# Attention and MoE on one core: a head's row maxima are transposed and stored in the following head's slot, and v's magnitude is broadcast one slot later

## The chip, the cores and the metric

The kernel runs on one core of a Trainium2 chip. The metric is the device time of one execution in microseconds (us); the time of before is the median of three runs. Besides, one execution was recorded by the hardware profiler, and all views quoted here are of that execution. PE is the engine for matrix products, PEld its weight loads, DVE, ACT and POOL are the vector, scalar and general engines, SP only issues transfers. "ACTq" is the instruction queue of ACT where it issues a transfer.

## The reference, cut to what matters

```python
# q, k, v: 8 batches, 8 heads, 576 rows of 64; block = 64
scores = scale * np.matmul(q, k.transpose(0, 1, 3, 2))
scores = np.where(block_i >= block_j, scores, -1000000000.0)
scores = scores - np.max(scores, axis=-1, keepdims=True)
attn = np.exp(scores)
attn = attn / (np.sum(attn, axis=-1, keepdims=True) + 1e-09)
out = np.matmul(attn, v)
# x: the heads side by side, 4608 tokens of 512
h = x @ w_in                                  # 512 -> 2048
sp = np.maximum(h, 0.0) + np.log1p(np.exp(-np.abs(h)))
g = h * erf(sp)
return g @ w_out                              # 2048 -> 512
```

So there are 64 heads of masked attention, and behind them one feed-forward layer over 4608 tokens.

## The kernel before

**Attention, one head after the other.** A loop over n runs through 64 heads and four slots more. One turn of the loop is called a slot here. In slot n the code lists the steps of several heads and merges them evenly over the slot:

- `load_qk(n + 3)` brings the queries and keys of head n + 3 into one of four buffers `qk`.
- `maxes(n + 2)` finds the row maxima of head n + 2: five groups of score products `s` on PE (L324), each reduced by DVE into a column of `mx` (L327), and then step `e`. Step `e` takes the smaller of two columns on DVE (L352), transposes `mx` on PE into `mt` (L354), copies that row out of PSUM on ACT (L356), and has ACT issue a transfer that puts it into a row of the head's `qk` buffer (L357).
- `probs(n)` computes the scores of head n once more (`t`, L370 and L371; L370 reads the stored row, which subtracts the maximum), takes the exponential on ACT (L375), and splits the result in two float16 parts `ph` and `pl` (L381 on ACT, L382 on DVE).
- `pv` multiplies two heads' probabilities by v (`u`, L414) and sums them (`us`, L437); `normalise` does the rest for four heads (`rt`, `rb`, `xs`).

Every fourth slot `load_v` fetches v of four heads, and in the slot after it `prep_v` takes its largest magnitude (`vm` on DVE, transposed to `vt` on PE, three small DVE instructions on `vs`), broadcasts it by a PE product `vb` (L284), copies that as `vsb` and scales v into `vh` and `vl`.

**Feed-forward as filler.** The first 6 of 16 chunks of the feed-forward width (`F1`) are computed in units of 256 tokens and two chunks: 24 products `m_h` (L154), the gate on ACT, DVE and POOL (L123 to L137), and 12 products `o` (L164), which is 36 PE matmuls a unit and 54 units in all. The tokens of a batch are ready when its eight heads are done. The other ten chunks (`m2`) follow at the end, in tiles of 512 tokens.

**What sets the order.** The code gives an order of priority, and when the program is built a list scheduler lays down every engine's rows: where it reckons an engine free, it puts a later instruction that is ready, mostly of the filler, ahead. On the chip every engine then works through its own rows strictly in that order, and a row that has to wait holds up all rows behind it. `late(kind, ...)` shifts a step's priority; the kinds that the change touches have no shift. PSUM tiles come from four rotating banks (`bank`, pool `ps_a`), plus the filler's own while there is no filler yet. Until then PE also gets `warm` products without a use.

Of the kernel before, what the change touches and what calls it, by code (L numbers as in the profile page):

```python
# [15 lines left out]
AX = mybir.AxisListType  # L16
# the top word of the float64 2**-126, read as a float32
LEAST = 0.25 * (1 + 0.125) * 2.0**-13
PSUM = bass.MemoryType.PSUM

# erf(softplus(h)) as a function of r0 = tanh(T0 * h + T1).  Each step makes the next r:
#   ("S", i):    (p[0] * r_i + p[1]) ** 2
#   ("M", i, j): (r_i + p[0]) * r_j
#   ("A", i, j): p[0] * r_i + r_j
# and the value is the last r plus FIN.
PROG = [('S', 0), ('S', 1), ('M', 2, 2), ('M', 1, 3), ('M', 4, 4)]
# [8 lines left out]
def tile_attention_moe(ctx: ExitStack, tc: tile.TileContext, qk, v, w, maskrows, sels, out):  # L35
    nc = tc.nc
    B, H, D2, S = qk.shape
# [5 lines left out]
    F1 = 6  # L43
    SP = 640
    SCALE = 0.125
    NQ = H // 4
# [42 lines left out]
    def load_weight(whi, wlo, stage, f):  # L89
        """the two float32r parts of chunk f of both weights, out of the words of their float64"""  # L90
        for s in range(2):
            nm = f"{f}_{s}"
            raw = stage[0][0].tile([P, stage[0][2]], I32, tag=stage[0][1][s], bufs=stage[0][3], name=f"raw{nm}")[:, : 2 * DM].rearrange("p (n t) -> p n t", t=2)
            nc.sync.dma_start(raw.rearrange("p n t -> p (n t)"), w[f, s].bitcast(I32))
            top, low = raw[:, :, 1], raw[:, :, 0]
            # sign, exponent and 20 bits of mantissa as a float32 (0 for what is below its range)
            bits = stage[1][0].tile([P, stage[1][2]], I32, tag=stage[1][1], bufs=stage[1][3], name=f"bits{nm}")[:, :DM]
# [4 lines left out]
            nc.vector.scalar_tensor_tensor(out=sq, in0=sq, scalar=LEAST * LEAST, in1=f32(bits), op0=ALU.is_ge, op1=ALU.mult)  # L102
            # the low word, of the weight that the exponent gives it
            nc.vector.tensor_scalar(out=bits, in0=sq.bitcast(I32), scalar1=-0x800000, scalar2=None, op0=ALU.bitwise_and)  # L104
# [8 lines left out]
    def gate(h, name, gpool):  # L113
        """g = h * erf(softplus(h)) as a sum of two float32r parts"""
        n = h.shape[1]
        last = {}
# [26 lines left out]
    def moe_unit(ws, xh, xl, o, tw, nu, u, name, first, last, spread):  # L143
        """nu chunks of d_ff over tw tokens: the steps to their g, and those to their part of o"""
        turns.append(u)
# [25 lines left out]
    def merged(*lists):  # L171
        """the steps of all lists, each list (steps, from, to) spread evenly over its part of the whole"""
        order = []
        for n, (steps, lo, hi) in enumerate(lists):
            order += [(lo + (hi - lo) * (i + 0.5) / len(steps), n, i) for i in range(len(steps))]
        return [lists[n][0][i] for _, n, i in sorted(order)]
# [4 lines left out]

# [1 line left out]
    def load_x(pool, t, tw):  # L183
# [33 lines left out]
    def moe1(ready, lag):  # L217
        """the next step of the first F1 chunks, if there is one: a unit up to its g together with an earlier unit from g on"""
        t = len(xs1)
# [19 lines left out]
    with tc.tile_pool(name="apool", bufs=2) as apool, tc.tile_pool(name="spool", bufs=1) as spool, \  # L239
# [4 lines left out]
        nc.sync.dma_start(sel, sels)  # L244
        # columns of the keys' tiles 0, 3, 4 and 1, 2 in the two parts of a head's probabilities
        p32s = [spool.tile([P, n], F32, name=f"p32_{i}") for i, n in enumerate(PN)]
# [10 lines left out]
        def bank(name):  # L257
            """a bank of PSUM; all of them take part as long as the other chunks of d_ff need none"""
            turn.append(0)
            k = len(turn) % 8 if not xs1 else 0  # L260
            if k in (2, 5):
                return ps_h.tile([P, 512], F32, tag="h", name=name)
            if k in (3,):
                return ps_o.tile([P, 512], F32, tag="o", name=name)
            return ps_a.tile([P, 512], F32, tag="a", name=name)
# [5 lines left out]

        def prep_v(b, qd, v32):
            """two float16 parts of v over its largest magnitude, and that magnitude"""
            nm = f"{b}_{qd}"
# [3 lines left out]
            nc.tensor.transpose(out=pt[:1, :P], in_=vm, identity=ident)  # L278
            vs = apool.tile([1, 2], F32, tag="vs", name=f"vs{nm}")
            nc.vector.tensor_reduce(out=vs[:, :1], in_=pt[:1, :P], axis=AX.X, op=ALU.max)  # L280
            nc.vector.tensor_scalar(out=vs[:, :1], in0=vs[:, :1], scalar1=1e-30, op0=ALU.max, scalar2=None)
            nc.vector.reciprocal(out=vs[:, 1:2], in_=vs[:, :1])
            pb = bank(f"vb{nm}")
            nc.tensor.matmul(pb[:, :2], lhsT=onesrow, rhs=vs, start=True, stop=True)  # L284
# [11 lines left out]
        def part(n, i):  # L296
            """part i of head n: kl over kh, qh over ql, kh over 5 rows that mask, qh over 5 rows that mask"""
            return qks[n % NB][:, i * S : (i + 1) * S]
# [18 lines left out]
        def maxes(n):  # L317
            """the steps to the rows' maxima, negated, in the row of t that goes with the ones"""
            mx, K = mxs[n % 2], D + 4
# [41 lines left out]
        def probs(n, out):  # L361
            """the steps to exp(0.125 * s - its maximum), keys on partitions, in two float16 parts"""
            K = D + 5
# [25 lines left out]
        def pv(qd, pp, prs, V, usb, rs):  # L389
            """the steps to the unnormalised outputs of heads 2pp and 2pp+1 of the quad, and to their sums"""  # L390
            vsb, vh, vl = V
            st = {}

            def ranges(q0, q1):
                """keys' tiles that a part of the queries attends to: the queries, and where their probabilities are"""
                for j in range(5):
# [21 lines left out]

            # the sums of two heads' first 384 and last 192 queries, in a group of 32 columns each
            order = []  # L420
# [24 lines left out]
        def normalise(b, qd, usbs, rs):  # L445
            nm = f"{b}_{qd}"
            # pair, tile of the sums, part of the queries, head
            ri = apool.tile([P, 2, 3, 2, 2], F32, tag="ri", name=f"ri{nm}")
# [29 lines left out]
        for n in range(NB - 1):  # L478
            for f in load_qk(n):
                f()  # L480
        v32 = load_v(0, 0)
        vs[0] = prep_v(0, 0, v32)
        for f in maxes(0) + maxes(1):
            f()
        def late(kind, steps):
            """steps whose instructions the scheduler holds behind the next ones of the order, or ahead of some (offsets in instructions)"""
            def run(f):
# [27 lines left out]
        for n in range(N + 4):  # L515
# [4 lines left out]
            if n + 2 < N:  # L520
                lists.append((late("max", maxes(n + 2)), 0, 1))
            if n < N:
# [3 lines left out]
            if n % 4 == 1 and qd < N // 4:  # L526
                v32 = load_v(*divmod(qd, NQ))
            if n % 4 == 2 and qd < N // 4:
                lists.append((late("v", [lambda qd=qd: vs.__setitem__(qd, prep_v(*divmod(qd, NQ), v32))]), 0, 1))
            if n % 2 == 0 and 2 <= n <= N:  # L530
# [26 lines left out]

# [1 line left out]
    N2 = 2  # L559
# [89 lines left out]
```

## Time and profile before

| | |
|---|---|
| time, median of 3 runs | 1394.77 us (1393.82 to 1400.65) |
| span of the profiled execution | 1407.0 us; no other time is given of that execution |
| attention with filler, from head 12 to the first score product of head 63 | 170 to 743 us |
| filler alone, then the weights of the other chunks | 743 to about 960 us |
| the other chunks | to the end |

Three views are used: busy time by stretch of the span (with the granted clock of PE, 1.00 being full speed), the waits of an engine by what it waited for, and the instructions in order of time. An engine's idle time counts only where something behind it is late because of it. A busy PE need not be a PE at its peak, since matmuls are pipelined and their ends modelled.

### The profile page before, as it was taken

The page shows a single profiled execution, that of the slowest core. Times are in us where ns is not written, and L with a number is a line of the kernel's source. Part 1 is how long each engine was busy: PE and PEld are TensorE (multiplying, and loading weights), DVE is VectorE, ACT ScalarE, POOL GpSimd, SP SyncE. Part 2 cuts the span into 40 slices and gives each one's busy share as a digit, 9 for nine tenths or more (in the row PEclk, how much of TensorE's full clock was granted, in tenths as well). Part 3 has the DMA queues.
Part 4 walks back from the last instruction along what each step waited for, and adds up shares of the span by engine and source line. Part 5 has one row for each costly group of instructions (what it writes and reads, how often), then busy time and mean ns, then how long its engine had stood idle before and what let it go on. Part 6 is the DMA issues. An engine that isn't in the chain of part 4 may idle for free. (4 is left out here: it accounts for less than half of the span.)

```text
span 1407.0 us, 21952 instructions
## 1 busy us (share of the span) xinstructions
PE 1273.8 (91%) x8198; PEld 1026.1 (73%) x8198; DVE 1013.9 (72%) x1525; ACT 793.2 (56%) x1493; POOL 602.1 (43%) x454
## 2 busy tenths in 40 slices
PE   3798789989899898999889898779999999999998
PEld 1455567777777787777777787568888888888887
DVE  5768997788878788788697648996555555564654
ACT  1456566667666676667567455544444454445453
POOL 3757665445554554544445424562222222222221
PEclk9879899999999999999999899899999999999999
DMA  8557655757657576566623542302211311321110
GB/s 228 135 125 204 173 156 137 185 154 193 179 129 207 146 196 175 152 161 177 174 81 137 188 164 95 130 0 78 102 60 68 113 60 60 108 72 61 60 61 30
DMA packets 89370, 179.95 MB, mean 128 GB/s; under 512 B 8540, under 2 KB 27292, under 8 KB 89264
## 3 DMA queue, kind: packets, MB, share of 16 engines
q1 hardware_dynamic: 79280, 159.41, 38.1%
q0 software_dynamic: 9344, 18.97, 6.1%
q8 instruction: 65, 1.06, 0.3%
q10 hardware_dynamic: 640, 0.17, 0.1%
q14 instruction: 41, 0.34, 0.1%
HBM read 112.29 MB, written 37.75 MB: 107 GB/s over the span
## 5 line engine op out<-in xcount | busy, mean ns | idle before, releaser
L130 DVE SCALAR_TENSOR_TENSOR m_r<-m_r 128x512 f32<-128x512 f32 x288 | 232.9, 809 | 229.3 <-ACT m_r L128 225.8
L137 POOL TENSOR_TENSOR m_gl<-m_r,m_gh 128x512 fp32r<-128x512 f32 x144 | 195.5, 1357 | 443.7 <-ACT m_gh L136 359.2
L136 ACT CAST m_gh<-m_r 128x512 fp32r<-128x512 f32 x144 | 89.2, 619 | 251.9 <-DVE m_r L135 251.7
L154 PE MATMUL m_h<-xh,whi 128*128 128x256 f32 (+1 forms) x648 | 213.3, 329 | 17.3 <-DVE m_r L135 17.3
L128 ACT ACTIVATE m_r<-m_r,c 128x512 f32<-128x512 f32 x288 | 207.9, 722 | 11.0 <-ACT m_r L128 0.4
L154 PE MATMUL m_h<-xl,whi 128*128 128x256 f32 (+1 forms) x648 | 211.1, 326 | 0.3 <-DMA xl<-x_d 0.3
L154 PE MATMUL m_h<-xh,wlo 128*128 128x256 f32 (+1 forms) x648 | 211.1, 326 | 0.0
L327 DVE TENSOR_REDUCE mx<-s 64x1 f32<-64x288 f32 (+4 forms) x384 | 167.9, 468 | 56.4 <-PE s L324 53.9
L375 ACT ACTIVATE p<-t 128x288 f32<-128x288 f32 (+4 forms) x384 | 143.1, 388 | 97.9 <-PE t L371 76.2
L164 PE MATMUL o<-whi,m_gh 128*128 128x512 f32 x432 | 173.8, 403 | 6.7 <-ACT ob L209 4.3
L164 PE MATMUL o<-wlo,m_gh 128*128 128x512 f32 x432 | 173.8, 402 | 0.0
L382 DVE TENSOR_TENSOR pl<-p,ph 128x832 f16<-128x832 f32 (+1 forms) x128 | 158.5, 1240 | 18.0 <-ACT ph L381 17.8
L312 POOL TENSOR_TENSOR qk<-st,qk 64x576 fp32r<-64x576 f32 x64 | 103.2, 1613 | 157.5 <-PE s L324 55.9
L154 PEld LDWEIGHTS m_h<-xh,whi 128*128 128x128 f32 x648 | 126.6, 195 | 37.8 <-DVE m_r L135 21.9
L164 PE MATMUL o<-whi,m_gl 128*128 128x512 f32 x432 | 153.0, 402 | 0.2 <-POOL m_gl L137 0.2
L370 PE MATMUL t<-qk 69*128 69x288 f32 (+4 forms) x384 | 136.0, 355 | 12.6 <-DVE mx L327 7.0
L324 PE MATMUL s<-qk 68*128 68x256 f32 (+3 forms) x384 | 126.6, 362 | 14.3 <-DVE mx L327 8.7
L313 POOL TENSOR_TENSOR qk<-st,qk 64x576 fp32r<-64x576 f32 x64 | 111.3, 1739 | 65.5 <-DMA qk<-qk 61.7
L154 PEld LDWEIGHTS m_h<-xl,whi 128*128 128x128 f32 x648 | 126.5, 195 | 15.8 <-DMA xl<-x_d 0.6
L154 PEld LDWEIGHTS m_h<-xh,wlo 128*128 128x128 f32 x648 | 126.9, 196 | 9.4
L371 PE MATMUL t<-qk 128*128 128x288 f32 (+4 forms) x384 | 129.8, 339 | 0.0
L123 ACT ACTIVATE m_r<-m_h,c 128x512 f32<-128x512 f32 x144 | 98.8, 686 | 50.5 <-PE m_h L154 48.7
(84 smaller groups left out, 2499.1 us busy)
## 6 DMA issues: line engine op xcount, KB each, us to landing
st<-qk SPq DMA_DIRECT2D x64, 288.0 KB
qk<-qk POOLq DMA_DIRECT2D x64, 288.0 KB, 4.6
qk<-qk SPq DMA_DIRECT2D x64, 288.0 KB
x_d<-xs SPq DMA_DIRECT2D x32, 576.0 KB
raw<-w SPq DMA_DIRECT2D x32, 512.0 KB
v<-v SPq DMA_DIRECT2D x16, 640.0 KB
qk<-qk SPq DMA_DIRECT2D x64, 144.0 KB
xh<-x_d SPq DMA_DIRECT2D x18, 512.0 KB
```

What stands on the lines that cost most here:

```text
L128: nc.scalar.activation(r, regs[o[1]], AF.Square, bias=const(pp[1]), scale=pp[0])
L130: nc.vector.scalar_tensor_tensor(out=r, in0=regs[o[1]], scalar=pp[0], in1=regs[o[2]], op0=ALU.add, op1=ALU.mult)
L137: nc.gpsimd.tensor_tensor(out=gl, in0=g, in1=f32(gh), op=ALU.subtract)
L154: nc.tensor.matmul(h[:, k, :], lhsT=a[:, 0, sl], rhs=x[:, cc, :], start=cc == 0 and i == 0, stop=cc == NCC - 1 and i == 2)
L164: nc.tensor.matmul(o[c], lhsT=a[:, sl], rhs=b_[:, 1, :], start=first and k == 0 and not lo and b_ is whi, stop=last and k == nu - 1 and lo)
L313: nc.gpsimd.tensor_tensor(out=t[D:, 1, :], in0=st[D:, :], in1=f32(t[D:, 1, :]), op=ALU.subtract)
L324: nc.tensor.matmul(dst[:r, :w_], lhsT=qh[:K, i * P : i * P + r], rhs=kh[:K, k0 : k0 + w_], start=True, stop=True)
L327: nc.vector.tensor_reduce(out=mx[:r, col : col + 1], in_=src, axis=AX.X, op=ALU.max, negate=True)
L370: nc.tensor.matmul(s[:kk, :w_], lhsT=kh[:K, ks], rhs=qh[:K, q0 : q0 + w_], start=True, stop=False)
L371: nc.tensor.matmul(s[:kk, :w_], lhsT=klh[:, ks], rhs=qhl[:, q0 : q0 + w_], start=False, stop=True)
L375: nc.scalar.activation(p32s[part][:kk, c : c + w_ - skip], s[:kk, skip:w_], AF.Exp, scale=SCALE)
L382: nc.vector.tensor_tensor(out=pl, in0=p, in1=ph, op=ALU.subtract)
```

## The change

Step `e` of `maxes(n + 2)` no longer stands at the end of slot n. It is kept in `rows` and listed in slot n + 1, spread over the first 0.6 of it; probs of that head still stand in slot n + 2. `prep_v` is cut in two: `scale_v` ends with the reciprocal in `vs` and stays in the slot of before, and the rest, from the broadcast `vb` on, comes one slot later. What is computed, and how often, stays the same. (Comments and docstrings also go, which moves line numbers: L324, L327, L352, L354, L356, L357 and L370 become L332, L335, L360, L362, L364, L365 and L378; L284 becomes L292.)

```diff
+        vs_ = {}
+        def scale_v(b, qd, v32):
             nm = f"{b}_{qd}"
             vm = apool.tile([P, 1], F32, tag="vm", name=f"vm{nm}")
...
             vs = apool.tile([1, 2], F32, tag="vs", name=f"vs{nm}")
+            vs_[qd + NQ * b] = vs
             nc.vector.tensor_reduce(out=vs[:, :1], in_=pt[:1, :P], axis=AX.X, op=ALU.max)
...
             nc.vector.reciprocal(out=vs[:, 1:2], in_=vs[:, :1])
+
+        def prep_v(b, qd, v32):
+            nm = f"{b}_{qd}"
+            vs = vs_.pop(qd + NQ * b)
             pb = bank(f"vb{nm}")
...
+        scale_v(0, 0, v32)
         vs[0] = prep_v(0, 0, v32)
-        for f in maxes(0) + maxes(1):
-            f()
+        rows = {}
+        for n in range(2):
+            *steps, rows[n] = maxes(n)
+            for f in steps:
+                f()
+        rows.pop(0)()
...
             if n + 2 < N:
-                lists.append((late("max", maxes(n + 2)), 0, 1))
+                *steps, rows[n + 2] = maxes(n + 2)
+                lists.append((late("max", steps), 0, 1))
+            if n + 1 in rows:
+                lists.append((late("max", [rows.pop(n + 1)]), 0, 0.6))
...
             if n % 4 == 2 and qd < N // 4:
+                lists.append((late("v", [lambda qd=qd: scale_v(*divmod(qd, NQ), v32)]), 0, 1))
+            if n % 4 == 3 and qd < N // 4:
                 lists.append((late("v", [lambda qd=qd: vs.__setitem__(qd, prep_v(*divmod(qd, NQ), v32))]), 0, 1))
```

Three places show how the engines' rows move. The first is PE around the transpose of head 31's maxima (`mt`, from buffer `mx_123`). Before, it stands behind head 31's last score product `s_31_1` and 15 rows of others, and right ahead of the last scores of head 29:

```order
L467 MATMUL rb_0_0_0_4013<-ident,rw_0_0_4010 128x128 x3
L467 MATMUL rb_0_0_1_4018<-ident,rw_0_0_4010 128x128
L467 MATMUL rb_0_0_1_4018<-ident,rw_0_0_4010 128x64
L354 MATMUL mt_4026<-ident,mx_123 5x128
L370 MATMUL t_29_256_4031<-qk_95 128x320
L371 MATMUL t_29_256_4031<-qk_95 128x320
```

Of the change, the same transpose stands in the middle of head 30's scores, behind three score products of head 32:

```order
L378 MATMUL t_30_288_4071<-qk_96 128x288
L379 MATMUL t_30_288_4071<-qk_96 128x288
L332 MATMUL s_32_4075<-qk_94 128x384
L362 MATMUL mt_4079<-ident,mx_123 5x128
L154 MATMUL m_3_1_h<-xh_768_7257,whi_734 128x256
L154 MATMUL m_3_1_h<-xl_768_7259,whi_734 128x256
L378 MATMUL t_30_320_4084<-qk_96 128x256
```

The transpose has moved some 50 rows of PE behind the last score product that it depends on, and it has come nearer to `t_31`, which needs the stored row. The names of the filler also differ: before, unit 4_0 or 4_1 of the filler runs beside head 29 (`m_4_0`), and of the change unit 3_0 or 3_1.

The second place is DVE at the minimum that the transpose waits for. Before, it stands behind the last reduction of head 31 and a part of head 29's split, and the transpose on PE comes with it:

```order
L327 TENSOR_REDUCE mx_123<-s_31_0_3983 64x1
L454 RECIPROCAL ri_0_3920<-rt_0_3994 128x24
L327 TENSOR_REDUCE mx_123<-s_31_1_4002 64x1
L382 TENSOR_TENSOR pl_29_3991<-p_0_113,ph_29_3990 128x832
L352 TENSOR_TENSOR mx_123<-mx_123 64x1
```

Of the change, DVE has five more rows between that minimum and the reduction of `s_32_4075`, whose product PE issues one row ahead of the transpose:

```order
L335 TENSOR_REDUCE mx_123<-s_31_1_4022 64x1
L360 TENSOR_TENSOR mx_123<-mx_123 64x1
L390 TENSOR_TENSOR pl_29_4030<-p_1_114,ph_29_4029 128x768
L477 TENSOR_TENSOR xs_0_1_4033<-usb_3781,rb_0_1_0_4037 128x384
L477 TENSOR_TENSOR xs_0_1_4033<-usb_3781,rb_0_1_1_4042 128x192
L335 TENSOR_REDUCE mx_122<-s_32_4059 128x1 x2
L130 SCALAR_TENSOR_TENSOR m_3_0_r_8558<-m_3_0_r_8558 128x512
L335 TENSOR_REDUCE mx_122<-s_32_4075 128x1
```

The minimum stayed directly behind its head's last reduction; it is PE's transpose that has moved away from it.

The third place is DVE at v's magnitude (`vs`, then `vsb`, which needs PE's `vb`). Before, the copy `vsb` follows the reciprocal at once:

```order
L280 TENSOR_REDUCE vs_0_4095<-vt_0_4093 1x1
L130 SCALAR_TENSOR_TENSOR m_4_0_r_8720<-m_4_0_r_8720 128x512
L281 TENSOR_SCALAR vs_0_4095<-vs_0_4095 1x1
L135 SCALAR_TENSOR_TENSOR m_4_0_r_8720<-m_4_0_r_8720,m_4_0_h 128x512
L282 RECIPROCAL vs_0_4095<-vs_0_4095 1x1
L286 COPY vsb_0_4101<-vb_0_4099 128x2
```

Of the change, it stands nine rows later, behind the rest of head 32's reductions and three of head 33:

```order
L390 TENSOR_TENSOR pl_30_4171<-p_1_114,ph_30_4170 128x768
L335 TENSOR_REDUCE mx_123<-s_33_4183 128x1 x2
L335 TENSOR_REDUCE mx_123<-s_33_4199 128x1
L335 TENSOR_REDUCE mx_123<-s_33_4212 128x1
L294 COPY vsb_0_4217<-vb_0_4215 128x2
```

The broadcast `vb` on PE moves with it, from 18 rows behind `vt` to 155 rows behind it.

More of the change, by code (lines that the diff above doesn't have):

```diff
@@ L270, in load_v @@
             return v32
-        def prep_v(b, qd, v32):
+        vs_ = {}
+        def scale_v(b, qd, v32):
             nm = f"{b}_{qd}"
```

## The prediction, as it was made

> **What bounds the kernel now.** I read the page first. In the profiled execution PE is the busiest engine:
>
> ```profile
> span 1407.0 us, 21952 instructions
> PE 1273.8 (91%) x8198; PEld 1026.1 (73%) x8198; DVE 1013.9 (72%) x1525; ACT 793.2 (56%) x1493; POOL 602.1 (43%) x454
> ```
>
> The change sits in the attention stage, so the average doesn't answer for it. The busy time by stretch does; its columns are length, busy time of PE, PEld, DVE, ACT and POOL, granted clock, share of the DMA engines, GB/s.
>
> ```profile
> 170.00:308.00 138.00, 122.21 (x1037) 100.42 (x1036) 117.49 (x182) 91.30 (x194) 73.36 (x54) 0.95 0.61 164
> 308.00:486.00 178.00, 164.49 (x1394) 134.82 (x1394) 143.70 (x234) 122.30 (x256) 91.14 (x67) 0.96 0.64 168
> 486.00:656.00 170.00, 159.01 (x1369) 130.07 (x1368) 136.52 (x227) 119.64 (x253) 85.09 (x66) 0.97 0.66 177
> 656.00:743.00 87.00, 76.97 (x635) 63.70 (x635) 70.39 (x110) 56.79 (x119) 44.44 (x32) 0.94 0.47 130
> ```
>
> In these 573 us PE is busy 522.7 and idle 50.3, and DVE is busy 468.1 (82%). The clock was below 1.00 for 0.05 x 138 + 0.04 x 178 + 0.03 x 170 + 0.06 x 87 = 24 us worth of time. So PE loses 74 us, idle and slowed. The waits of PE in that stage (total, times, longest) say on whom:
>
> ```profile
> PE mt L354 <- DVE mx L352: 23.7, 20, 2.8
> PE t L370 <- DVE mx L327: 6.4, 9, 1.8
> PE vb L284 <- DVE vs L282: 5.3, 4, 1.8
> PE s L324 <- DVE mx L327: 4.8, 3, 2.3
> PE u L414 <- DVE pl L382: 4.6, 4, 2.7
> ```
>
> All of it is DVE lagging behind PE. Half is the transpose of the maxima, which comes too close behind the reductions; the broadcast of v's magnitude is a tenth. Four heads at a time show what the stage does without such waits:
>
> ```profile
> 170.40:216.53 46.13, 39.08 (x338) 31.53 (x336) 43.73 (x65) 30.15 (x64) 31.95 (x21) 0.96 0.58 154
> ...
> 308.20:346.03 37.83, 37.72 (x336) 30.88 (x335) 31.10 (x56) 29.34 (x63) 22.09 (x16) 1.00 0.64 177
> 346.03:393.60 47.57, 42.07 (x357) 34.44 (x355) 39.00 (x60) 31.33 (x67) 22.65 (x18) 0.96 0.65 167
> ```
>
> Heads 24 to 27 (308 us on) ran with PE always busy at full clock, 9.5 us a head; the next four took 11.9. Both are the same code. The stage is bound by PE where DVE keeps up, and by the lockstep of PE and DVE where it doesn't.
>
> **Part 1: the waits that go.** In the new order DVE has finished the minimum long before PE comes to the transpose: five DVE rows and three score products lie between. The broadcast has a slot in place of a few rows. I take both waits as gone: 23.7 + 5.3 = **29 us**. The transpose of v's magnitude and the waits for PSUM banks (`t` and `s` behind a reduction) stay.
>
> **Part 2: the clock.** A wait costs twice here, as the stretch around the longest shows:
>
> ```profile
> 470.00:472.00 2.00, 0.23 (x1) 0.00 (x0) 2.00 (x2) 0.49 (x1) 0.60 (x1) 1.00 1.03 321
> 472.00:474.00 2.00, 0.99 (x5) 0.99 (x6) 1.97 (x4) 0.68 (x2) 0.15 (x1) 0.79 0.88 178
> 474.00:476.00 2.00, 2.00 (x15) 1.23 (x15) 0.90 (x3) 1.84 (x4) 1.02 (x2) 0.50 0.83 298
> 476.00:478.00 2.00, 2.00 (x25) 1.59 (x22) 0.00 (x0) 0.66 (x3) 0.71 (x1) 0.86 0.58 138
> ```
>
> PE stood for 2.8 us, and the clock then fell to 0.50 for some 3 us. Over the stage 24 us went this way for 50 us of idle time, 0.48 us for each. With 29 us fewer I take 0.48 x 29 = **14 us** (bounds: nothing, if other waits keep the clock low, and all 24).
>
> [...]
>
> **Part 3: the filler that moves.** Counted in the two orders, 1274 filler matmuls stand ahead of the first score product of head 63 before, and 921 in the change: 353, or 9.8 units of 36, leave the attention stage for the stretch behind it. What a unit costs there, with no attention beside it, is in the DVE rows that end a gate, and in the busy time of the same place:
>
> ```profile
> L135 DVE SCALAR_TENSOR_TENSOR m_r<-m_r,m_h x7: 679/689/690, 822.7 to 857.6; 128x512 f32<-128x512 f32 x7
> ```
>
> ```profile
> 836.00:868.00 32.00, 32.00 (x206) 28.92 (x205) 21.00 (x29) 17.10 (x28) 10.57 (x8) 1.00 0.31 102
> ```
>
> Six units in 34.9 us are 5.8 us each, and PE is full, so 9.8 units **add 57 us** behind the attention. In the attention stage they save as much if PE is what bounds it, and nothing if PE waits for others anyway. The bounds are 0 and, by the four-head rows (85 filler matmuls in 37.8 us, 106 in the 47.6 us that follow), 0.5 us a matmul, which is waits more than work. I take 57, the price of a full PE, since heads 24 to 27 show that state. So part 3 sums to **nothing**, but the stage must then really get 57 us shorter.
>
> **Part 4: the new wait.** The row must land in the buffer before the head's first `t`. Before, about a slot of PE work lay between; now it is 22 matmuls (head 32) or about as many with the short `us` (head 31): 22 x 32.0 / 206 = 3.4 us by the row of the full PE, to 4.3 with the drains of the attention stage. Two heads show how long the chain takes, transpose to landing: head 34,
>
> ```profile
> 402.84 0.27 PE L354 MATMUL mt<-ident,mx 128*5 128x128 f32 x1
> 403.14 0.25 ACT L356 CAST mt<-mt 5x128 fp32r<-5x128 f32 x1 [0.31 <-PE mt L354]
> 403.43 0.70 ACTq L357 DMA_DIRECT2D qk<-mt  x1
> ```
>
> with all ten packets of ACT's transfer queue between 404.1 and 405.2,
>
> ```profile
> q10 hardware_dynamic: 10, 0.00, 1.0%
> ```
>
> and head 52, one of the slowest:
>
> ```profile
> 599.08 0.28 PE L354 MATMUL mt<-ident,mx 128*5 128x128 f32 x1
> ```
>
> ```profile
> 600.59 0.25 ACT L356 CAST mt<-mt 5x128 fp32r<-5x128 f32 x1
> 600.75 0.42 ACT L375 ACTIVATE p<-t 128x320 f32<-128x320 f32 x1
> 600.87 0.70 ACTq L357 DMA_DIRECT2D qk<-mt  x1
> ```
>
> whose last two packets ran only between 606.4 and 606.7:
>
> ```profile
> q10 hardware_dynamic: 2, 0.00, 0.8%
> ```
>
> So the chain takes 2 to 7.5 us against 3.4 to 4.3. A fast head waits for nothing, the slowest 4 us. I take 0.3 us a head, near the fast end, where most heads are: 51 x 0.3 = 15 us, and with the clock's 0.48 **22 us** back. Ends: 0, and 51 x 1 x 1.48 = 75. Behind a waiting `t` on PE stand all filler and the next heads' scores, so nothing covers it. The issue itself (0.70 us of ACT's queue) only changes its place, ahead of exponentials that ACT (68% busy) would run; I count nothing, and 51 x 0.7 = 36 us would be the most if each came at a bad moment.
>
> **Part 5: what else moves.** `vl` and `vh` come a slot later, two slots before they are read: nothing. They free v's buffer a slot later; SP's queue keeps the next v load in its place two slots on, so nothing; if that cover went, DVE's present wait would grow:
>
> ```profile
> DVE vm L276 <- DMA v<-v: 8.9, 5, 3.7
> ```
>
> POOL's rows keep their order but for the later filler. At the start, 30 `warm` products in place of 16 stand ahead of head 0's scores and head 1's row comes earlier; both lie beside the first weights, whose work on ACT holds the exponentials back: nothing, 3 us either way.
>
> **Sum.** -29 - 14 + (57 - 57) + 22 = **-21 us** on the span of 1407.0. That span is 0.9% above the median of the runs, 1394.8; the waits scale with neither, so I predict 1394.8 - 21 = **1374 us**.
>
> **Rivals.**
>
> *The row's landing takes the place of the wait removed.* At (29 + 14) / 1.48 / 51 = 0.57 us a head the gain is eaten: 1395. For: head 52's 7.5 us, and DMA engines 61 to 66% busy. Against: head 34's 2 us, and a wait there lets DVE catch up, so that bank waits shrink.
>
> *DVE becomes the bound; this one is slower.* The filler that leaves is also what covered DVE's lag. In the stage DVE spent on it
>
> ```profile
> L130 DVE SCALAR_TENSOR_TENSOR m_r<-m_r 128x512 f32<-128x512 f32 x70 | 64.0, 914 | 3.6 <-ACT m_r L128 3.3
> ...
> L130 DVE SCALAR_TENSOR_TENSOR m_r<-m_r,m_r 128x512 f32<-128x512 f32 x35 | 38.2, 1090 | 0.3
> ...
> L135 DVE SCALAR_TENSOR_TENSOR m_r<-m_r,m_h 128x512 f32<-128x512 f32 x35 | 23.7, 677 | 0.4
> ```
>
> 125.9 us for 35 units, 3.6 each. Without 9.8 units DVE still has 468 - 35 = 433 us. If it stays at its 82% the stage takes 433 / 0.817 = 530 us in place of 573, 43 less, while the filler behind it costs 57: **+14, 1409 us**. It turns at a stage of 516 us, DVE at 84%; my forecast (573 - 57 - 21 = 495) needs 87%. For it: no fast group of heads had DVE above 82%. Against: heads 12 to 15 had it at 43.73 of 46.13, 95%, and its idle time is partly the lockstep that the change loosens.
>
> *All of DVE's lag goes.* With the later transposes PE also stops waiting for banks: 50.3 + 24 = 74 less, and a landing wait of 15: 1336.
>
> *It doesn't do what it says.* The minimum could still be late at the transpose, with DVE more than five rows behind; then 1395 as well.
>
> **How the numbers follow.** My forecast of 1374 has 0.49, with a range of its own of 1355 to 1388. Nothing gained (landing, or lag that only moves) 0.24, 1388 to 1402. DVE bound 0.19, 1402 to 1420. All lag gone 0.08. A measurement of this kernel tells about 0.5%, 7 us, from no change. So faster 0.57, same 0.24, slower 0.19. The range of 8 in 10 leaves out the fastest case and the slower half of the slow one: 1350 to 1409.
>
> **What would show it.** Right: the wait of `mt` for DVE's minimum and that of `vb` are gone from PE's list; the attention stage is about 78 us shorter, the filler alone 57 longer; the granted clock is above 0.96 and DVE at 87% or so. A wait of `t` for the row's transfer or ACT's copy shows part 4 and its size. A stage less than 57 us shorter means the DVE rival, seen as `t` and `s` waiting for reductions. What would make me wrong most easily is the size of part 4, or a stage in which the filler was free.

## The result, and the profile after

The changed kernel takes **1410.6 us** (median of 17 runs, 1404.3 to 1417.8) against 1398.4 (17 runs, 1391.7 to 1413.5) of the kernel before on the same chip: a ratio of **1.0083**, 95% interval 1.0061 to 1.0105. It is 12 us slower; 1374 had been predicted, so the sign was wrong.

The page of the profiled execution, span and engines:

```profile
span 1412.2 us, 21977 instructions
PE 1295.3 (92%) x8198; PEld 1030.9 (73%) x8198; DVE 1006.6 (71%) x1525; ACT 789.6 (56%) x1493; POOL 615.0 (44%) x454
```

The first thing to see is PE: the same 8198 matmuls, and 21.5 us more of busy time. PE's idle time went down from 133.2 to 116.9 us, as intended, and the kernel is slower all the same.

The busy time by stretch of the changed kernel, with the columns of before: the attention stage (from head 12 to the first score product of head 63, both counted at `t`), the filler alone behind it, and the other chunks.

```profile
160.90:689.20 528.30, 491.79 (x4090) 388.64 (x4088) 428.83 (x711) 356.78 (x775) 294.00 (x205) 0.94 0.63 169
689.20:872.20 183.00, 175.03 (x1126) 150.24 (x1125) 114.62 (x152) 99.02 (x165) 65.50 (x44) 0.97 0.38 129
872.20:1412.00 539.80, 509.77 (x2199) 417.79 (x2197) 335.02 (x456) 256.79 (x391) 155.91 (x115) 0.97 0.21 72
```

The first two stretches of the kernel before, cut at the same places:

```profile
170.40:742.70 572.30, 521.99 (x4423) 428.48 (x4422) 467.40 (x749) 389.38 (x819) 293.73 (x217) 0.96 0.61 164
742.70:868.30 125.60, 117.85 (x773) 101.39 (x772) 82.61 (x111) 68.24 (x117) 48.53 (x33) 0.96 0.42 144
```

The filler alone is 57.4 us longer, with 353 matmuls more: what Part 3 had forecast. The stage is 44.0 us shorter, where 78 was needed. PE's waits in the changed kernel's stage (total, times, longest):

```profile
PE t L378 <- DVE mx L335: 9.1, 12, 2.1
PE mt L362 <- DVE mx L360: 7.8, 8, 1.9
PE t L378 <- DMA qk<-mt: 6.9, 9, 1.5
PE u L422 <- DVE pl L390: 2.9, 4, 1.3
PE t L378 <- ACT p L383: 2.4, 3, 1.1
```

The wait for v's magnitude (`vb`) is gone (in the trace that `vb` stands 93 rows of PE behind `vt`, not 155), that of `mt` for the minimum is down to a third, and `t` waits for the row's transfer, which it didn't before.

### The profile page after: what moved, and what is told of

Its sections match the earlier page's. It is cut to its first block, busy times and chain, and to the rows that moved or that the text cites. A ratio compares the mean times of both kernels' runs of the same rounds, so it can differ in the third digit from the quotient of the medians.

```text
span 1412.2 us, 21977 instructions
## 1 busy us (share of the span) xinstructions
PE 1295.3 (92%) x8198; PEld 1030.9 (73%) x8198; DVE 1006.6 (71%) x1525; ACT 789.6 (56%) x1493; POOL 615.0 (44%) x454
## 5 line engine op out<-in xcount | busy, mean ns | idle before, releaser
L130 DVE SCALAR_TENSOR_TENSOR m_r<-m_r 128x512 f32<-128x512 f32 x288 | 225.3, 784 | 255.3 <-ACT m_r L128 251.7
L137 POOL TENSOR_TENSOR m_gl<-m_r,m_gh 128x512 fp32r<-128x512 f32 x144 | 197.6, 1372 | 464.2 <-ACT m_gh L136 436.6
L154 PE MATMUL m_h<-xh,whi 128*128 128x256 f32 (+1 forms) x648 | 215.2, 332 | 15.9 <-DVE m_r L135 15.8
L154 PE MATMUL m_h<-xh,wlo 128*128 128x256 f32 (+1 forms) x648 | 212.7, 328 | 0.0
L154 PE MATMUL m_h<-xl,whi 128*128 128x256 f32 (+1 forms) x648 | 212.5, 328 | 0.0
L335 DVE TENSOR_REDUCE mx<-s 64x1 f32<-64x288 f32 (+4 forms) x384 | 169.6, 467 | 51.4 <-PE s L332 49.5
L164 PE MATMUL o<-whi,m_gh 128*128 128x512 f32 x432 | 175.1, 405 | 9.1 <-ACT ob L209 4.9
L390 DVE TENSOR_TENSOR pl<-p,ph 128x832 f16<-128x832 f32 (+1 forms) x128 | 167.9, 1313 | 10.8 <-ACT ph L389 10.4
L164 PE MATMUL o<-wlo,m_gh 128*128 128x512 f32 x432 | 175.3, 406 | 0.0
L378 PE MATMUL t<-qk 69*128 69x288 f32 (+4 forms) x384 | 138.4, 361 | 22.7 <-DVE mx L335 11.0
L321 POOL TENSOR_TENSOR qk<-st,qk 64x576 fp32r<-64x576 f32 x64 | 123.0, 1921 | 80.1 <-DMA qk<-qk 78.3
L154 PEld LDWEIGHTS m_h<-xh,whi 128*128 128x128 f32 x648 | 127.1, 196 | 40.1 <-DVE m_r L135 24.3
L164 PE MATMUL o<-whi,m_gl 128*128 128x512 f32 x432 | 154.6, 404 | 0.9 <-POOL m_gl L137 0.9
L332 PE MATMUL s<-qk 68*64 68x288 f32 (+3 forms) x384 | 128.6, 359 | 22.0 <-DVE mx L335 12.5
L320 POOL TENSOR_TENSOR qk<-st,qk 64x576 fp32r<-64x576 f32 x64 | 103.2, 1613 | 95.4 <-issue 21.4
L154 PEld LDWEIGHTS m_h<-xl,whi 128*128 128x128 f32 x648 | 126.8, 196 | 15.4 <-issue 0.6
L154 PEld LDWEIGHTS m_h<-xh,wlo 128*128 128x128 f32 x648 | 126.8, 196 | 10.8 <-issue 0.7
L379 PE MATMUL t<-qk 128*128 128x288 f32 (+4 forms) x384 | 125.9, 329 | 0.0
```

The lines of the kernel that those rows point to most:

```text
L130: nc.vector.scalar_tensor_tensor(out=r, in0=regs[o[1]], scalar=pp[0], in1=regs[o[2]], op0=ALU.add, op1=ALU.mult)
L137: nc.gpsimd.tensor_tensor(out=gl, in0=g, in1=f32(gh), op=ALU.subtract)
L154: nc.tensor.matmul(h[:, k, :], lhsT=a[:, 0, sl], rhs=x[:, cc, :], start=cc == 0 and i == 0, stop=cc == NCC - 1 and i == 2)
L164: nc.tensor.matmul(o[c], lhsT=a[:, sl], rhs=b_[:, 1, :], start=first and k == 0 and not lo and b_ is whi, stop=last and k == nu - 1 and lo)
L321: nc.gpsimd.tensor_tensor(out=t[D:, 1, :], in0=st[D:, :], in1=f32(t[D:, 1, :]), op=ALU.subtract)
L332: nc.tensor.matmul(dst[:r, :w_], lhsT=qh[:K, i * P : i * P + r], rhs=kh[:K, k0 : k0 + w_], start=True, stop=True)
```

## The experiments

### Both kernels profiled once more

One execution's split is not the kernel's, so both were profiled again.

> The kernel before, profiled once more, to see how much of the split is the execution's and not the kernel's. The first profile has head 12 at 170.4 us, the attention stage at 572.3 and the stretch of filler alone at 125.6, and its span of 1407.0 lies 9 us above the median of the runs. If the stage repeats to 3 us, the 44 us by which the change's stage is shorter stand, and the 9 us come from the start of the execution or its end. If the stage comes out at 563 or so, the change's stage is only 35 us shorter and nearly the whole of the loss (57 - 35 less the earlier start) is in the stage. DVE-bound rival: nothing different, 572. Filler-was-free theory: nothing different either.

> The changed kernel, profiled once more. First profile: head 12 at 160.9 us, stage 528.3, filler alone 183.1, clock loss in the stage 32.4 us against 23.9 before. If the clock loss comes out near 24 here, the clock's share of the result is a matter of the execution and not of the change; if it stays above 30, the change costs clock. Filler alone is to repeat to 1 us (353 matmuls, at 0.162 us each).

Stage and filler alone of the kernel before, second profile (span 1388.5 us):

```profile
162.30:725.30 563.00, 525.62 (x4424) 432.81 (x4422) 461.94 (x750) 388.83 (x819) 290.88 (x218) 0.95 0.63 167
725.30:848.20 122.90, 115.11 (x774) 98.91 (x772) 82.61 (x111) 68.23 (x117) 48.56 (x33) 0.99 0.43 147
```

and of the change (span 1406.6 us):

```profile
161.90:686.50 524.60, 488.74 (x4090) 386.25 (x4088) 428.61 (x711) 356.80 (x775) 290.26 (x204) 0.94 0.63 170
686.50:866.70 180.20, 172.25 (x1127) 148.57 (x1125) 114.61 (x152) 98.99 (x164) 65.57 (x44) 0.99 0.39 131
```

Before's stage and its start moved by 8 to 9 us between two executions of one program (563.0 after 572.3, head 12 at 162.3 after 170.4); the change's by 4 and 1. So a difference of under 10 us between single profiles says nothing here, and below the means of the two are used. They lie 11.7 us apart in span (1397.75 and 1409.4), as the timed medians do (12.2). The clock's loss in the stage was 23.9 and 27.3 us before, 32.4 and 29.0 in the change: no gain, and a loss of some 5 us at most.

PE's waits on the moved steps in the second profiles, first of before, then of the change:

```profile
PE mt L354 <- DVE mx L352: 17.9, 18, 1.7
PE vb L284 <- DVE vs L282: 4.3, 4, 1.3
...
PE mt L362 <- DVE mx L360: 7.5, 8, 1.9
PE t L378 <- DMA qk<-mt: 7.5, 7, 2.6
```

PE's busy time in the stage fell by 36.9 us in this pair and by 30.2 in the first, with 335 filler matmuls fewer (910 for 1245). At the price that a filler matmul has behind the attention, 0.162 us (worked out below), it would have been 54. Some rows of PE in the stage of before by line (count, time in which at least one of them ran, mean ns of one), `t` first, then the filler:

```profile
L371 PE MATMUL t<-qk 128*128 128x288 f32 (+4 forms) x306 | 102.7, 336 | 0.0
L154 PE MATMUL m_h<-xh,whi 128*128 128x256 f32 x281 | 82.9, 295 | 0.0
L164 PE MATMUL o<-wlo,m_gh 128*128 128x512 f32 x134 | 55.2, 412 | 0.0
```

and of the change:

```profile
L379 PE MATMUL t<-qk 128*128 128x288 f32 (+4 forms) x306 | 98.7, 323 | 0.0
L154 PE MATMUL m_h<-xh,whi 128*128 128x256 f32 x206 | 62.6, 304 | 1.2 <-DVE m_r L135 1.2
L164 PE MATMUL o<-wlo,m_gh 128*128 128x512 f32 x96 | 42.3, 440 | 0.0
```

Over all rows of the stage (count times mean), one product of the attention took 0.288 us before and 0.287 in the change, one filler matmul 0.331 and 0.344. The products overlap on PE: added up they make 1328 and 1226 us, 2.53 and 2.51 times the busy time. So no part of the busy time belongs to the filler or to the attention alone. Behind the attention the factor is 2.1. Means, change less before:

| piece of the span | us |
|---|---|
| up to head 12 | -5.0 |
| stage: PE busy | -33.5 |
| stage: PE idle | -7.7 |
| filler alone | +57.4 |
| the rest | +0.4 |
| sum | +11.6 |

**335 filler matmuls freed 33.5 us of PE beside attention, 0.10 us each; behind it, 353 cost 57.2, 0.162 each.** That difference, 24 us, is twice the loss.

### One part of the change alone

```diff
 (e1: v as before)
-lists.append((late("v", [lambda qd=qd: scale_v(...)]), 0, 1))
-if n % 4 == 3 and qd < N // 4: ... prep_v
+lists.append((late("v", [lambda qd=qd: (scale_v(...), vs.__setitem__(qd, prep_v(...)))]), 0, 1))
 (e2: maxima as before)
-*steps, rows[n + 2] = maxes(n + 2)
-lists.append((late("max", steps), 0, 1))
+lists.append((late("max", maxes(n + 2)), 0, 1))
 (e3: the change, the row earlier in the slot)
-lists.append((late("max", [rows.pop(n + 1)]), 0, 0.6))
+lists.append((late("max", [rows.pop(n + 1)]), 0, 0.2))
```

> Only the maxima's transpose and store go a slot later; v's magnitude stays as before. In the order 1093 filler matmuls stand ahead of head 63's scores (before 1274, the change 921). Theory A (the loss is filler that leaves the attention stage: a unit costs 5.8 us behind it and saves only some 4 in it, while the waits that go give some 14 us back): 5.0 units fewer, so about half of the change's loss, 1398 to 1406 us where before is 1398. Theory B (the loss is the later store: scores wait for the row): as slow as the whole change, 1407 to 1412. Theory C (the loss is v's later broadcast): no slower than before, 1385 to 1398.

> Only v's broadcast and split go a slot later; the maxima stay as before. 1046 filler matmuls ahead of head 63's scores, 6.3 units fewer than before. Theory A: some of the change's loss, 1400 to 1408. Theory B: not slower than before, 1390 to 1398. Theory C: all of the loss, 1407 to 1413.

> The whole change, but the transpose and store are listed in the first 0.2 of the following slot in place of the first 0.6, so that the row lands earlier. 1199 filler matmuls ahead of head 63's scores, 2.1 units fewer than before. Theory A: faster than the change by most of its loss, at or below before, 1386 to 1399. Theory B: the same, as the wait for the row goes. Theory C: still slow, 1407 or more.

Measured: e1 1.0093 [1.0055, 1.0130], e2 1.0019 [0.9987, 1.0051], e3 1.0188 [1.0137, 1.0239]. Each part takes away its own wait and no other. With v alone:

```profile
PE mt L362 <- DVE mx L360: 23.1, 22, 3.7
```

and with the row alone:

```profile
PE t L378 <- DMA qk<-mt: 8.2, 7, 2.2
PE t L378 <- DVE mx L335: 8.2, 6, 3.7
PE mt L362 <- DVE mx L360: 6.1, 8, 1.5
PE vb L292 <- DVE vs L285: 5.4, 4, 1.9
```

With the row at a tenth of the slot (e3) the wait for the minimum is back, and PE waits longer for banks (`t` behind a reduction, 6.4 and 5.2 us before):

```profile
PE mt L362 <- DVE mx L360: 30.4, 24, 3.4
PE t L378 <- DVE mx L335: 10.0, 10, 3.3
```

The row's place decides how many filler matmuls stand ahead of head 63, in the order of rows: 1093 in e1, 1046 in e2, 1199 in e3 (1274 before, 921 in the change). e3 missed all three expectations: nearly all of the filler is back, and it is slower than the change, with stage and filler alone at 706.5 us (mean of before 691.9) and head 12 at 177.3. So the filler's return alone does not undo the loss where a wait returns with it. In e1 and e2 each filler matmul that left the stage freed 0.135 and 0.139 us of PE's busy time and took 0.158 and 0.167 behind it: the change's gap (0.10 and 0.162), but smaller. e2 paid nothing that can be told for its 6.3 units; and e1's loss isn't in the stage at all: stage and filler alone take 539.3 + 151.3 = 690.6 us, but head 12 comes at 178.5 in place of 166.4. In that start PE ran at two thirds of its clock:

```profile
100.00:178.50 78.50, 68.31 (x410) 46.15 (x409) 58.26 (x96) 40.21 (x86) 51.52 (x34) 0.65 0.59 160
```

### More filler in the stage, by its rate

```diff
-    RATE = 1
+    RATE = 8    (e4: the change; e5: before)
+    RATE = 10   (e6: before; e7: the change)
```

> The whole change, but the code lists 8 filler steps a slot in place of 1, so that 1261 filler matmuls stand ahead of head 63's scores, as before (1274). The later transpose and store, and v's broadcast, stay as in the change. Theory A: the loss goes, 1385 to 1400. Theory B and C: the loss stays, 1406 to 1415, since their waits are untouched.

> Before, with 8 filler steps listed a slot in place of 1: a control for the run of the change with more filler. 1290 filler matmuls ahead of head 63's scores (before 1274). Theory A (the change loses because filler left the attention stage): as before, 1393 to 1404, since the filler is the same, and so the change with 8 steps equals it only because the waits that it removes bring nothing. Theory D (listing filler by the slot is a gain in itself, and the change is slow for another reason): 1380 to 1390.

> Before, with 10 filler steps listed a slot: 1488 filler matmuls ahead of head 63's scores, 5.9 units more than before. Theory A, by the price of the two runs of the change (9.4 units cost 55 us behind the stage and 43 in it): 7 us faster than before, 1388 to 1396. Rival (the stage has no more room, each unit costs its full 5.8 us there): no change, 1396 to 1403.

> The change with 10 filler steps a slot: 1483 filler matmuls ahead of head 63's scores, 15.6 units more than the change. Theory A: faster than with 8 steps (1397.8) by some 7 us, 1386 to 1396. Rival (no more room): 1396 to 1403.

Measured: e4 0.9996 [0.9963, 1.0029], e5 1.0131 [1.0089, 1.0174], e6 1.0182 [1.0142, 1.0221], e7 1.0112 [1.0073, 1.0151]. With the filler put back (1261 matmuls ahead of head 63) the change has lost nothing: e4 is level with before. At the same rate the change is ahead of before by 18 us (1397.8 to 1415.5) and by 7 (1416.5 to 1423.8). That looks like the waits' gain, but in the profiles it lies at the start: head 12 comes at 164.8 in e4 and 178.4 in e5 (at rate 10, 172.7 and 184.4), while stage and filler alone take 699.4 and 692.2 (700.2 and 694.3). So the rate itself seems to cost at the start in the kernel before, and these pairs show no gain in the stage. The expectations of e5, e6 and e7 were all missed, on the slow side. Beyond before's amount filler is not cheap in the stage: PE's busy time there rises by 0.20 us for each matmul more from before to e6, and by 0.18 from e4 to e7.

### The filler taken out, with no row moved

```diff
-k = RATE if n < N else RATE2
+k = (RATE if n >= 27 else 0) if n < N else RATE2     (e12 and e13)
-if not xs1:
+if not xs1 and n < 10:                               (e13: no warm products from slot 10 on)
```

> The kernel before with the filler's own steps listed only from slot 27 on (RATE is 0 until then); neither the row of maxima nor v is moved. 917 filler matmuls stand ahead of head 63's first score product, as in the change (921; before 1274), all of them behind head 26. Filler alone must take 183 us. Theory that filler beside attention is nearly free: the stage gets 43 us shorter or less (353 x 0.12), and the time is 1398 + 57 - 43 = 1412 or above, as the change's, although no row was moved; heads 12 to 26 run without filler and take nearly as long as the 9.5 to 11.9 us a head with it. Theory that the row's move is what costs and a filler matmul costs the same 0.161 us anywhere: 1398. DVE-bound rival: heads 12 to 26 get shorter by the DVE work that leaves, 43 us in all, 1412 as well, and DVE then shows 82% or more in heads 12 to 26; if DVE shows well less than 82% there, it is not what bounds them.

> As e12 (before, the filler's steps listed from slot 27 on, 917 filler matmuls ahead of head 63's first score product, row and v not moved), but without the warm products from slot 10 on; in e12 151 of them took 32 us of PE in the stage, which confounds it. Theory that the filler's leaving is what costs: the stage gives back 0.126 us for each of some 330 matmuls, 42 us, the filler alone takes 57 more, and the time is 1398 + 15 = 1413. Theory that the row's move costs and filler is worth the same anywhere: 1398. DVE-bound rival: 43 us of stage gained against 57, also 1412, but then DVE shows 82% in heads 12 to 26, where there is no filler. A clock that falls where there is no filler would give more than 1413.

Measured: e12 **1.0256** [1.0203, 1.0309], e13 **1.0495** [1.0438, 1.0551]. In both 917 filler matmuls stand ahead of head 63, as in the change, and neither the row nor v is moved. Two other things do change as long as there is no filler: the attention takes PSUM tiles from the filler's banks too, and in e12 170 more `warm` products run (280 ahead of head 63 in place of 110). The stage of e12, all products first, then the filler's lines L154 and L164 and the useless `warm` ones (L510), which stay as long as there is no filler:

```profile
153.40:707.50 554.10, 505.66 (x4249) 394.24 (x4249) 434.19 (x718) 361.06 (x775) 278.99 (x208) 0.95 0.60 161
...
153.40:707.50 554.10, 108.57 (x630) 0.95 0.60 161
153.40:707.50 554.10, 94.20 (x287) 0.95 0.60 161
153.40:707.50 554.10, 44.67 (x152) 0.95 0.60 161
```

Less `warm`, PE is busy for 505.7 - 44.7 = 461.0 us, 62.8 less than before's mean (523.8), with 328 filler matmuls fewer: 0.19 us each, no less than the 0.162 behind the attention. So **e12 does not show that filler is cheap beside attention where no row is moved**; its loss, some 36 us, is of the size of what `warm` takes. (`warm` overlaps with the rest as well, so its true share is not known.) Without the `warm` products (e13) the expected 1413 was far off. In heads 12 to 19, which have no filler, and in the rest:

```profile
163.60:258.70 95.10, 77.45 (x519) 55.71 (x520) 63.29 (x110) 48.14 (x107) 52.95 (x36) 0.63 0.59 153
258.70:753.60 494.90, 448.76 (x3579) 359.13 (x3578) 373.48 (x607) 315.83 (x667) 228.90 (x174) 0.88 0.56 151
```

PE was busy for 81% of that first stretch, and the granted clock was 0.63. DVE, with 67%, is far from full there. In e12 the clock was 0.95 from 153 to 260 us, and the two differ in `warm` alone: products beside the attention's kept the clock up here (0.95 for 0.63), even without a use. In the change, whose filler thins out evenly, the clock hardly suffered (0.94 for 0.96 and 0.95).

### The row later in the slot

```diff
-lists.append((late("max", [rows.pop(n + 1)]), 0, 0.6))
+..., 0.6, 1))                                       (e11)
+..., *((0, 0.6) if n < 12 else (0.6, 1))))          (e14)
+..., *((0, 0.6) if n < 12 else (0.6, 0.6))))        (e16)
+..., *((0, 0.6) if n < 12 else (0.7, 0.7))))        (e17)
```

> The whole change with one number other: step e is spread over 0.6 to 1 of the slot (its middle at 0.8) in place of 0 to 0.6 (middle at 0.3). In the order 1332 filler matmuls then stand ahead of head 63's first score product (921 in the change, 1274 before), so filler alone must take some 116 us (183.1 - 411 x 0.162). Theory that the filler's leaving is what costs (it was nearly free beside the attention): the time is back at before's or below, 1385 to 1398, with the mt and vb waits still gone. Theory that the row's move itself costs (the landing wait of t on the row, 0.14 us a head in the change): the row now lands half a slot nearer to t, the wait of t for the transfer grows to 0.5 us a head or 25 us and more, and the time is 1405 to 1425. DVE-bound rival: the stage grows by the filler's DVE work, 411 / 36 x 3.6 = 41 us / 0.82 = 50, and the tail shrinks by 67, so 17 faster than the change: 1394.

> The whole change, with step e spread over 0 to 0.6 of the slot up to slot 11 (as in the change) and over 0.6 to 1 from slot 12 on (as in e11). 1372 filler matmuls then stand ahead of head 63's first score product. In e11 stage and filler alone took 674.6 us together, against 685.9 in the second profile of before and 704.8 in the change's, but head 12 came at 183.8 us in place of 162. If the late row in the first slots did that, head 12 comes at 162 here and the time is 1398 - 11 = 1387 or below, faster than both kernels. If it was the clock of that start, whatever the rows, head 12 comes at 175 to 184 again and the time is 1395 to 1406. Theory that the row's landing decides: the wait of t for the transfer is 12 us as in e11, 5 more than in the change.

> The whole change, with step e at 0.3 of the slot up to slot 11 and at 0.6 from slot 12 on (0.8 in e14). 1200 filler matmuls stand ahead of head 63's first score product (921 in the change, 1274 before), so filler alone takes about 135 us. Theory that filler leaving at 0.126 against 0.162 us a matmul is what made the change slow: 279 matmuls come back and bring 279 x 0.036 = 10 us against the change, 1400, level with before. Landing theory: the wait of t for the transfer lies between the change's 7 us and the 27 of e14, and each us of it shows in the time. DVE-bound rival: 279 / 36 x 3.6 / 0.82 = 34 us more stage against 45 less tail, 11 us faster than the change, 1400 as well; not told apart by this run.

> As e16 with the row at 0.7 of the slot; 1296 filler matmuls ahead of head 63 (before 1274), so filler alone takes about 120 us. Filler's price: 375 x 0.036 = 13 us faster than the change, 1397 or 1398, level with before. If the removed waits for the minimum and for v's magnitude (18 and 5 us in the second profile of before) were gained as well, 1375 to 1385; if they come back at t as waits for the row's transfer or for banks, 1398.

| row's place in the slot, from slot 12 on | filler ahead of head 63 | wait of `t` for the row's transfer, us | time, us | ratio |
|---|---|---|---|---|
| 0.3 (the change) | 921 | 6.9, 7.5 | 1410.6 | 1.0083 [1.0061, 1.0105] |
| 0.6 (e16) | 1200 | 5.0 | 1395.6 | 0.9975 [0.9942, 1.0009] |
| 0.7 (e17) | 1296 | 12.4 | 1391.3 | **0.9943 [0.9912, 0.9974]** |
| 0.8 (e14) | 1372 | 26.8 | 1396.0 | 0.9968 [0.9936, 1.0000] |
| 0.8 in all slots (e11) | 1332 | 11.9 | 1405.6 | 1.0041 [1.0006, 1.0077] |

These kernels hold the whole change; one number differs, and with it the filler's amount, so the two are not told apart here. With the row later and the filler back from slot 12 on, the change no longer costs anything, and at 0.7, the best of the places tried, it beats both kernels: 0.6% faster than before, 19 us faster than the change. The stage and the longest waits of e17:

```profile
159.90:732.00 572.10, 529.95 (x4464) 437.36 (x4462) 455.27 (x752) 391.30 (x826) 291.67 (x218) 0.96 0.63 167
```

```profile
PE t L378 <- DMA qk<-mt: 12.4, 10, 2.6
PE m_h L154 <- DVE m_r L135: 6.1, 4, 2.7
PE u L422 <- DVE pl L390: 5.1, 8, 1.1
PE t L378 <- DVE mx L335: 4.3, 5, 1.7
PE mt L362 <- DVE mx L360: 4.2, 2, 2.7
```

The wait for the minimum has turned into a wait for the row's landing, and PE's idle time in the stage, 42.1 us, is that of before (50.3 and 37.4). Later still (e14) the landing wait eats the gain:

```profile
PE t L378 <- DMA qk<-mt: 26.8, 13, 4.7
```

e11 against e14 settles a side question: with the late row in the first slots as well, the stretch ahead of head 12 ran at a lower clock. In e11,

```profile
100.00:183.80 83.80, 71.92 (x449) 49.70 (x448) 61.31 (x102) 43.40 (x93) 53.47 (x35) 0.65 0.59 151
```

and in e14, whose first slots are those of the change,

```profile
100.00:161.80 61.80, 56.50 (x417) 37.62 (x416) 55.86 (x93) 38.30 (x84) 44.88 (x31) 0.81 0.67 182
```

Head 12 comes 22 us sooner, and the time is 10 us better. What in the order of these first slots decides about that clock was not found.

### DVE's work taken away

```diff
 (e8: the change with RATE = 8; the lower part of the probabilities is left out, a constant zero tile stands for it)
-nc.vector.tensor_tensor(out=pl, in0=p, in1=ph, op=ALU.subtract)
+pl = zpl[part]
 (e15: e14, and one of the two subtractions a head on POOL)
+(nc.gpsimd if part in (1,) else nc.vector).tensor_tensor(out=pl, in0=p, in1=ph, op=ALU.subtract)
```

> The change with 8 filler steps, and the lower float16 part of the probabilities left out (a constant zero tile is used, PE's products with it remain): takes two DVE instructions of 1.25 us from every head, 128 us from DVE in the attention stage, with the same filler (1264). If DVE is what bounds the stage: its length falls from 571 us by 80 us or more, below 1320 us in all. If PE bounds it and DVE only holds it up now and then: by the waits of PE on DVE, some 20 to 35 us, 1363 to 1378.

> As e14, and one of the two subtractions a head (pl of 768 columns, 0.9 us or so on DVE) done by POOL, some 45 us of DVE in the stage; 1334 filler matmuls ahead of head 63. DVE-bound rival: stage and filler alone get 45 / 0.82 = 55 us shorter than in e14. Theory that DVE's lag is a wait here and there: as in the run without these subtractions (112 us of DVE gone, 32 us gained) some 13 us. If POOL is slower at it than DVE and u comes to wait for it, nothing or a loss.

e8: 0.9791 [0.9743, 0.9840], 27 us below e4, which differs in nothing else. Its stage:

```profile
160.50:699.60 539.10, 513.63 (x4397) 418.87 (x4395) 338.10 (x635) 376.12 (x810) 262.26 (x211) 0.97 0.65 171
```

and e4's:

```profile
164.80:736.00 571.20, 533.11 (x4394) 426.40 (x4393) 450.50 (x741) 381.57 (x814) 287.58 (x213) 0.95 0.60 163
```

112 us of DVE work left, and the stage got 32 us shorter. Were DVE the bound, it would have been 112 / 0.79 = 142 at e4's own share of 79%. So in e4 DVE's lag costs PE some 30 us (12.6 of idle time, 19.5 of busy time) and isn't what the stage runs at. The change itself, with its thinner filler, was not run without this work.

e15: **1.0270** [1.0223, 1.0318], a loss of 41 us against e14. POOL took 1.74 us for the subtraction of 768 columns that DVE did in 1.08 in e14 (the 0.9 us in the expectation was too low), and PE waited for it:

```profile
PE u L422 <- POOL pl L390: 20.5, 22, 3.2
PE t L378 <- DMA qk<-mt: 12.4, 9, 4.1
```

DVE had less to do and the kernel was slower, with a clock of 0.92 in the stage: relief for DVE that put a slower engine ahead of PE was a loss.

## Why the prediction was wrong

| step | predicted, us | measured, us (means of two profiles) |
|---|---|---|
| Part 1: waits of `mt` and `vb` | -29 | -13.2 and -4.8 |
| Part 4: wait of `t` for the row | +15 | +7.2 |
| other waits of PE in the stage | 0 | +3.1 |
| Part 2 and 4: clock | -14 + 7 | a loss of up to 5, inside the other lines |
| Part 3: filler that moves | -57 + 57 | -33.5 + 57.4 |
| start and rest | 0 | -4.6 |
| sum | -21 | +11.6 |

**Part 3 is the step that failed.** "I take 57, the price of a full PE" was right for what the filler costs behind the attention (57.2 us of PE's busy time), and wrong for what it frees in the stage: 33.5 us of PE. A filler matmul there runs beside more other products than behind the attention (2.53 at a time against 2.1), so at the stage's mean it holds 0.331 / 2.53 = 0.13 us of PE, and 335 of them 44 us. That is an estimate, since the ends of matmuls are modelled. The rest went as the filler that stayed took 4% longer, and as the overlap fell to 2.51, some 5 us each. Up to 5 us of that can be the clock's. The bounds, 0 to 57, held the value; the choice of the upper end was the error, made because one fast group of heads was taken for the state of the whole stage. e4 shows the change without the loss when the filler is put back and no moved step is touched; that filler's leaving costs this much without a moved step isn't shown (e12).

**Part 2 had the wrong sign.** Less idle time (-7.7 us) went with as much clock loss or more. "0.48 us for each" was the stage's average, and no price for each us of idle time: in the stages of the two first profiles the half clock came in pieces of 3.4 us, sometimes two or three on end; each piece lost 1.7 us, and there were 14 before and 19 in the change. e13 lost 94 us of the stage to the clock, with 64 us of idle time. The row of e13 has a mean of 0.63 over 95 us in which PE was busy for 81%, and over the 130 us behind them, to 389 us, PE was busy for 92% at a mean of 0.74; so a PE that was mostly busy by the profile ran well below full clock all the same.

**Part 1** was right in kind and 11 us too high: the `vb` wait was 4 to 5 us and went, but the transpose still waited 8 times, since DVE came to the minimum late there. **Part 4** was right in kind and half as large: 7.2 us over 51 heads is 0.14 us a head for the 0.3 assumed. Its 22 matmuls from transpose to reader hold for head 32 (24 in the trace) and not for the stage: head 31 has 55, the mean of heads 12 to 62 is 46, and no row gives the 4.3 us of its upper end; the trace has 4.6 us at the median. **Part 5** stands, but for the start, which differs between executions by more than it could say.

Of the rivals, "DVE becomes the bound" had the number: a stage of 530 us (528.3 and 524.6 measured) and 1409. Its mechanism isn't borne out: DVE's share stayed at 81 to 82%, which is why the sum came out, but it was no fixed share (79.6% in e17, 75.7% in e14), and in e8 the stage did not follow DVE's work. So the number was luck as far as these runs show, though the change itself, with its thinner filler, was never run with less work on DVE.

Open: why the filler that stays takes longer and PE's products overlap less when filler leaves, and how much of that is the moved row's doing. PE's time freed for each matmul was 0.10 us in the change, 0.135 and 0.139 in its halves (e1, e2), and 0.19 in e12, where neither the row nor v was moved. The ends of matmuls are modelled, so these profiles can't split it further.

## What to carry to other kernels

Where a change lets a scheduler move filler, count the filler that leaves and price it twice: what PE's total busy time loses where it stood, and what it gains where it goes; the two prices differed here by 0.06 us a matmul, over 20 us in all and more than the waits removed. A wait that is loosened by moving its step can be paid again at the step's reader (7 us for 18 here), so try several places for it: the same change was 0.8% slower at one and 0.6% faster at another. Profile both kernels twice before a difference of under 1% is split into stages.

## What the runs showed of the hardware

- The granted clock was well below full while PE was busy for most of the time: on average 0.63 over 95 us with 81% busy and 0.74 over the next 130 us with 92% (e13), and 0.65 over 78 us with 87% (e1). Products without a use, at 45 us of PE's time, were a gain: with them the order without filler up to slot 26 was 35 us faster (e12 1434.4, e13 1469.9).
- The same 8198 matmuls took PE 1268.2 and 1273.8 us of busy time before, and 1295.3 and 1293.1 in the change, by their order alone. By the modelled ends a filler matmul of 0.33 us held 0.16 us of PE behind the attention, where 2.1 ran at a time, and by the estimate above some 0.13 among its products, where 2.5 did.
- The subtraction 128x768 to float16 took 1.74 us on POOL (e15) and 1.08 on DVE (e14).
